# Attention followed by a two-branch maxout layer: wide loads for a second batch, masks by matmul for the first, and scores of two steps issued together

## The chip, the cores and the metric

The kernel runs on one core of one Trainium2 chip. The metric is the device time in microseconds (us), as the median of several executions. "Span" is the time from the first to the last instruction of one profiled execution. Every kernel here computes correct results, and the ratios compare its fast runs alone; a run counts as slow when it is over 1.5% above the fastest of the same kernel.

In the lines of the profile, PE is TensorE (matmuls) and PEld its weight loads, DVE is VectorE, ACT ScalarE, POOL GpSimd, and SPq the queue in which SyncE issues DMAs. PEclk, the granted clock, is the share of TensorE's full clock that it was given. PSUM is the memory into which matmuls write. L522 is line 522 of the kernel.

## The reference, cut to what matters

```python
# q, k, v: 4 batches x 8 heads x 768 tokens x 64; heads 0, 2, 6 are "retrieval" heads
scores = q @ k.T / sqrt(64)
mask   = causal                                        # retrieval heads
mask   = causal & (key < 4 | query - key < 64)         # the five streaming heads
a      = softmax(where(mask, scores, -1e9))
x      = (a @ v) with the heads side by side           # 3072 tokens x 512
out    = maximum(x @ w1, x @ w2) @ w_out               # 512 -> 1024 -> 512
```

## The kernel before

The maxout is rewritten as relu(x(w1 - w2)) w_out + x(w2 w_out). `wd` is the weight difference and `wm` the weight product, both made once on the chip. Four stages run for each batch: loads and transposes of q and k, attention for four pairs of heads, a transpose of the result, and the dense layer. A planner in Python (a list scheduler with estimated costs) fixes, before the program is built, the order in which each engine issues its work. So the order is static, and changing an estimate or a buffer count can reorder everything behind it.

q and k of batch 0 are loaded "wide" (six consecutive tokens a partition) and transposed on TensorE. Later batches are loaded narrow and transposed by the DMA:

```python
order, rate = ("(p n)", 0.34) if b == 0 and src is not v else ("(n p)", 0.225)
... nc.sync.dma_start(out=t.t[:, h], in_=src[b, head].rearrange(f"o {order} d -> p (o n) d", p=128))
...
if b > 0:
    tk.append(P.op(lambda e: nc.sync.dma_start_transpose(out=qk.t..., in_=qb.t...), {"SP": XBAR}, cast, ...))
```

Scores of one step of a pair of heads use 64 rows of the array, one head in the upper and one in the lower half, so that both stream at once. All else uses 128 rows. The exp runs on ScalarE and the mask is multiplied in on VectorE:

```python
for st in range(max(map(len, plans))):
    sc = Buf(sc_p)                                   # 2 buffers of two PSUM banks
    def score(e, ...):
        ... nc.tensor.matmul(sc.t[:, h, off:off + w], lhsT=qk.t[64*h:64*h+64, 1, ...],
                             rhs=qk.t[64*h:64*h+64, 0, q0:q0 + w], start=True, stop=True, ...)
    so.rows = 64
    ... nc.scalar.activation(out=view(a.t...), in_=view(sc.t...), func=ACT.Exp, scale=scale, ...)
    ... V.tensor_mul(out=x, in0=x, in1=m)            # the mask
    ... nc.tensor.matmul(po[h].t[...], lhsT=a.t[...], rhs=vb.t[:, h, j, :], ...)   # values
```

A dense result goes from PSUM through one of three result buffers to memory. The store is issued by the same in-order queue (SyncE) as all loads and all transposing DMAs:

```python
ot_t = tl("ot", [128, d_model], F32, 3)
...
o = P.op(lambda e, bk=bk, ot=ot: copy(e, ot.t, bk.t[:, 0]), {"ACT": 0.53, "DVE": 0.69}, ...)
P.op(lambda e, ot=ot, r0=r0: nc.sync.dma_start(out=out[r0:r0 + 128, :], in_=ot.t), {"SP": 0.45}, [o], [ot], prio=-10, ...)
```

Of the kernel before, what the change touches and what calls it, by code (L numbers as in the profile page):

```python
# [17 lines left out]
class Op:  # L18
    __slots__ = ("emit", "cost", "deps", "bufs", "prio", "size", "rate", "left", "users",
                 "ready", "engine", "start", "end", "done", "rows", "then")  # L20

    def __init__(self, emit, cost, deps, bufs, prio, size, rate):
        self.emit, self.cost, self.deps, self.bufs = emit, cost, deps, bufs
        self.prio, self.size, self.rate = prio, size, rate
        self.left = 0
        self.users = []
        self.ready = 0.0
        self.engine = self.start = self.end = self.done = None
        self.rows, self.then = 128, None
# [24 lines left out]
class Plan:  # L54
# [12 lines left out]
    def schedule(self):  # L67
# [3 lines left out]
        dma = 0.0  # L71
# [26 lines left out]
        while todo:  # L98
# [23 lines left out]
            if e == "PE":  # L122
                o.end += SWITCH if o.rows != rows else 0.0
                rows = o.rows
# [32 lines left out]
W_PRIO = 2.5  # L157
XBAR = 2.6
# [3 lines left out]
def kernel(  # L162
# [69 lines left out]
    warm = tl("warm", [128, 1], F32)  # L232
    tri = tl("tri", [128, 128])
    smk = tl("smk", [128, 448 + 320])
    w2_bf = tl("w2_bf", [128, KC, d_ff])
# [27 lines left out]
    gt_t = [old(2, 1, FC, GT), old(0, 0, FC, GT), old(0, 1, FC, GT)]  # L263
# [11 lines left out]
    def load_weight(name, c):  # L275
        dst, arr, n = {"w1": (w_raw[0], moe_w1, KC // 4), "w2": (w_raw[1], moe_w2, KC // 4),
                       "wo": (w_raw[2], moe_w_out, FC // 4)}[name]
        nc.sync.dma_start(out=dst[:, c * n:(c + 1) * n, :],
                          in_=arr[c * 128 * n:(c + 1) * 128 * n, :].rearrange("(c p) f -> p c f", p=128))

    EARLY = (("wo", 0), ("wo", 1), ("wo", 2), ("wo", 3), ("w2", 0), ("w2", 1))
    with tc.manual_schedule():
# [9 lines left out]
        nc.scalar.activation(out=warm, in_=one[:, 0:1], func=ACT.Exp, scale=1.0, bias=0.0)  # L292
# [51 lines left out]
    def run(full, head, col, exact):  # L344
# [7 lines left out]
        if exact:  # L352
# [5 lines left out]
            c_m = P.op(f, {"DVE": 1.0}, prio=-20)  # L358
# [13 lines left out]
        for i, name in enumerate(("w2", "w1")):  # L372
            for c in range(4):
                d_w[name, c] = None if (name, c) in EARLY else P.op(
                    lambda e, name=name, c=c: load_weight(name, c), {"SP": 0.5},
                    prio=W_PRIO + 0.1 * i + 0.01 * c, size=0.524, rate=0.36)
        wd_ops, w2_ops, wo_ops, wm_ops, w2t_ops = [], [], [], [], []
        for c in range(4):
            w2_ops.append(P.op(lambda e, c=c: copy(e, w2_bf[:, c, :], w_raw[1][:, c, :]),
                               {"DVE": 0.62, "ACT": 0.95}, [d_w["w2", c]], prio=40 + c))  # L380
# [3 lines left out]
        for c in range(4):  # L384
            def f(e, c=c):
                (V if e == "DVE" else nc.gpsimd).tensor_sub(
                    out=wd_bf[:, c, :], in0=w_raw[0][:, c, :], in1=w_raw[1][:, c, :])
            wd_ops.append(P.op(f, {"DVE": 1.3, "POOL": 2.4}, [d_w["w1", c], d_w["w2", c]], prio=48 + c))
        for fch in range(FC):
# [7 lines left out]
            o = P.op(tr, {"PE": 0.23}, w2_ops, [bk], prio=300 + fch)  # L397
# [52 lines left out]

        def attend(b, p, qk, vb, tk, ov, sink, r):
# [12 lines left out]
            for st in range(max(map(len, plans))):  # L464
                hs = [h for h in range(2) if st < len(plans[h])]
                pr = r + 0.1 * st
                steps = {h: plans[h][st] for h in hs}
                same = len(hs) == 2 and plans[0] is plans[1]
                sc = Buf(sc_p)
                at = Buf(as_p[st] if plans[hs[0]] is BAND else at_p)  # L470
                at2 = Buf(as_p[st]) if len(hs) == 2 and not same else at
                where = {hs[0]: at, hs[-1]: at2}

                def score(e, hs=hs, steps=steps, sc=sc):
                    for i in range(max(len(steps[h][1]) for h in hs)):
                        for h in hs:
                            if i < len(steps[h][1]):
                                j, q0, w, off = steps[h][1][i]
                                nc.tensor.matmul(sc.t[:, h, off:off + w],  # L479
                                                 lhsT=qk.t[64 * h:64 * h + 64, 1, j * 128:(j + 1) * 128],  # L480
                                                 rhs=qk.t[64 * h:64 * h + 64, 0, q0:q0 + w],
                                                 start=True, stop=True, skip_group_check=True)
                cols = max(sum(g[2] for g in steps[h][1]) for h in hs)
                so = score_op(score, cols / 2400 + 0.01, tk, [qk, sc], pr)
                so.rows = 64
                ready = {}
                for group in ([hs] if same else [[h] for h in hs]):
                    h0, nh = group[0], len(group)
                    kind, segs, n, diag = steps[h0]
                    a = where[h0]  # L490
                    view, n = region(kind, n)
                    pointer = kind in ("far", "far0")
                    deps = [so] + ([c_m] if pointer else [])
                    for one_ in ([[h] for h in group] if pointer else [group]):
                        def ex(e, a=a, sc=sc, h=one_[0], m=len(one_), view=view, kind=kind):
                            bias = {"far0": bias_0, "far": bias_j}.get(kind)
                            nc.scalar.activation(out=view(a.t[:, h:h + m]), in_=view(sc.t[:, h:h + m]),  # L497
                                                 func=ACT.Exp, scale=scale,
                                                 bias=0.0 if bias is None else bias[:, s0 + h:s0 + h + 1])
                        o = exp_op(ex, n * len(one_), pointer, deps, [sc, a], pr)  # L500
                        ready.update({h: [o] for h in one_})
                    if not pointer:
                        def mk(e, a=a, h0=h0, nh=nh, kind=kind, diag=diag):
                            for x, m in mask_pieces(kind, diag, a.t[:, h0:h0 + nh], nh, s0 + h0):
                                V.tensor_mul(out=x, in0=x, in1=m)  # L505
                        w = (128 * len(diag) if kind == "tri" else n) * nh
                        o = P.op(mk, {"DVE": w * 0.00056 + 0.2}, [o, c_m], [a], prio=pr)
                        ready.update({h: [o] for h in group})
                for h in hs:
                    def av(e, h=h, a=where[h], segs=steps[h][1]):  # L510
                        for (j, q0, w, off) in segs:
                            for t in range(-(-w // 128)):
                                i = q0 // 128 + t
                                nc.tensor.matmul(po[h].t[:, 0, i * (D + 1):(i + 1) * (D + 1)],  # L514
                                                 lhsT=a.t[:, h, off + t * 128:off + (t + 1) * 128],
                                                 rhs=vb.t[:, h, j, :], **flag_of(h))
                    n_av = sum(-(-g[2] // 128) for g in steps[h][1])
                    prev[h] = P.op(av, {"PE": 0.031 * n_av}, ready[h] + [prev[h], ov], [where[h], vb] + (po if prev[h] is None else [po[h]]),
                                   prio=100 + pr)
                if st == 2 and sink is not None:  # L520
                    sunk = sink()
            out_ops = []  # L522
            for h in range(2):
                if not full[s0 + h]:
                    ats, vs, o = sunk
# [6 lines left out]
                    prev[h] = P.op(av, {"PE": 0.13}, [o, prev[h]], [ats, po[h], vs], prio=100 + r + 0.7)  # L532
# [13 lines left out]
        def blk(t):  # L546
            return t.rearrange("c (n p) -> c p n", p=128)

        def pair(b, p):
# [5 lines left out]
            for i, src in enumerate((q, k, v)):  # L555
                t = Buf(ld)
                raws.append(t)
                order, rate = ("(p n)", 0.34) if b == 0 and src is not v else ("(n p)", 0.225)
# [10 lines left out]
            for i in range(2):  # L569
# [3 lines left out]
                cast.append(P.op(f, {"POOL": 0.95, "DVE": 0.62} if r < 1 else {"POOL": 0.95}, loads[i],  # L573
                                 [raws[i], qb], prio=r + 0.01 * i))
                if b > 0:
# [9 lines left out]
                tk.append(P.op(lambda e, bk=bk, i=i: copy(e, tok(qk.t[:, i]), blk(bk.t[:, 0].bitcast(BF16)[:, 0:S])),  # L585
                               {"DVE": 0.95, "ACT": 0.8}, [o], [bk, qk], prio=r))
            if b > 0:
# [7 lines left out]
            ov = P.op(fv, {"POOL": 0.95}, loads[2],  # L595
# [3 lines left out]
            if not (full[s0] and full[s0 + 1]):  # L599
                ks, vs, sc, ats = Buf(ks_p), Buf(vs_p), Buf(sc_p), Buf(sk_p)  # L600
# [11 lines left out]
                def sink():  # L612
                    o = score_op(lambda e: nc.tensor.matmul(sc.t[:, 0, 0:S - 256], lhsT=ks.t, rhs=qk.t[:, 0, 256:S],
                                                            start=True, stop=True, skip_group_check=True),
# [142 lines left out]
```

## Time and profile before

| | before |
|---|---|
| median of the 3 runs | 213.56 us (212.2 to 213.75) |
| span of the profiled run, mean granted TensorE clock | 211.9 us, 0.932 |
| first matmul, last matmul | 13.46 us, 204.8 us |
| TensorE busy | 176.6 us (83%) |

The busy line of the profile's page (engine, busy us, share of the span, instructions) and the first line of its chain of work that ended last (share of the span by engine):

```profile
PE 176.6 (83%) x1460; PEld 94.4 (45%) x1460; DVE 80.1 (38%) x202; ACT 115.9 (55%) x196; POOL 68.2 (32%) x161
...
PE 69%; DVE 8%; ACT 4%; issue 4%; DVEq 0%; ACTq 0%
```

Over the whole span no other engine comes near TensorE, and the chain runs through TensorE for two thirds of the time. A share of 83% hides, however, that the missing 17% lie in three places (start, an early thin stretch, one dip) and that "busy" time at a slow clock also counts as busy. The prediction takes these apart by stretches.

### The profile page before, as it was taken

What the parts mean: (1) busy time and instruction counts of PE and PEld (TensorE: products, weight loads), DVE (VectorE), ACT (ScalarE), POOL (GpSimd) and SP (SyncE); (2) the same over time, 40 slices, a digit from 0 to 9 for tenths busy, and PEclk for the clock granted to TensorE, in tenths of its full rate; (3) what the DMA queues carried; (4) which work ended last, traced back from release to release, by engine and by line L of the source; (5) the groups of instructions that cost most, each with busy time, mean ns of one, the idle gap of its engine ahead of it and who ended that gap; (6) DMA issues with size and microseconds to landing.
All of it is one profiled execution on the core that took longest, in us unless ns stands there. A gap on an engine that the chain in (4) does not pass through costs nothing.

```text
span 211.9 us, 4178 instructions
## 1 busy us (share of the span) xinstructions
PE 176.6 (83%) x1460; PEld 94.4 (45%) x1460; DVE 80.1 (38%) x202; ACT 115.9 (55%) x196; POOL 68.2 (32%) x161
## 2 busy tenths in 40 slices
PE   0038864689799999997879999999999999999960
PEld 0024641545445446545455454545554554545420
DVE  6523799935524563515662035364700000000000
ACT  2088894137385875649553476878472442725320
POOL 6007769929801476243282406120000000000000
PEclk9999996599999999999556999999999999999995
DMA  5999999999999999999999999951183202112030
GB/s 167 404 321 314 357 391 246 221 200 227 209 180 209 236 178 247 242 203 225 192 260 235 232 180 218 212 120 54 49 152 101 99 0 99 53 49 99 14 114 34
DMA packets 99118, 38.91 MB, mean 184 GB/s; under 512 B 91920, under 2 KB 93968, under 8 KB 99088
## 3 DMA queue, kind: packets, MB, share of 16 engines
q1 hardware_dynamic: 99088, 38.55, 82.2%
q8 instruction: 13, 0.21, 0.4%
q14 instruction: 17, 0.14, 0.2%
HBM read 25.17 MB, written 6.29 MB: 148 GB/s over the span
## 4 chain that ended last, share of the span: by engine, by line
PE 69%; DVE 8%; ACT 4%; issue 4%; DVEq 0%; ACTq 0%
PE mm L655 15%; PE mm L673 12%; PE po L514 6%; PE sc L479 6%; PE mm L679 6%; PE po L673 5%; PE sc L655 3%; PE mm L406 3%; DVE at L505 3%; PE po L655 2%; PE po L679 2%; PE sc L673 2%; DVE as_all L505 2%; ACT at L497 2%; ACT as_all L497 2%
## 5 line engine op out<-in xcount | busy, mean ns | idle before, releaser
L497 ACT ACTIVATE at<-sc 128x1024 bf16<-128x1024 f32 (+3 forms) x48 | 33.7, 743 | 7.1 <-PE sc L479 6.5
L655 PE MATMUL mm<-xt,wd_bf 128*128 128x384 bf16 x180 | 35.1, 338 | 0.1
L273 POOL CAST qb<-ld 128x384 bf16<-128x384 f32 x60 | 32.1, 573 | 3.8 <-DMA ld<-in_q_dram 2.0
L655 PEld LDWEIGHTS <-wd_bf 128*128 128x128 bf16 x256 | 24.8, 100 | 18.9 <-issue 4.3
L497 ACT ACTIVATE as_all<-sc 128x896 bf16<-128x896 f32 (+5 forms) x36 | 24.5, 711 | 8.9 <-PE sc L479 8.7
L673 PE MATMUL mm<-wo_bf,raw 128*128 128x512 bf16 x120 | 29.4, 379 | 0.0
L273 POOL CAST vb<-ld 128x384 bf16<-128x384 f32 x32 | 16.2, 533 | 38.6 <-PE po L514 17.1
L505 DVE TENSOR_TENSOR as_all<-as_all,smk 128x384 bf16<-128x384 bf16 (+4 forms) x44 | 20.8, 498 | 20.6 <-ACT as_all L497 20.1
L479 PE MATMUL sc<-qk 64*128 64x192 bf16 (+4 forms) x216 | 25.0, 295 | 2.9 <-ACT as_all L497 1.2
L673 PEld LDWEIGHTS <-raw 128*128 128x128 bf16 x192 | 17.7, 98 | 19.6 <-issue 0.7
L662 ACT ACTIVATE raw<-mm 128x384 bf16<-128x384 f32 x37 | 18.2, 493 | 12.5 <-PE mm L655 11.5
L505 DVE TENSOR_TENSOR at<-at,tri 128x256 bf16<-128x256 bf16 (+1 forms) x48 | 17.1, 364 | 17.4 <-ACT at L497 17.3
L514 PE MATMUL po<-vb,at 128*128 128x65 bf16 x252 | 15.8, 204 | 4.3 <-DVE at L505 4.3
L271 ACT COPY ot<-mm 128x512 f32<-128x512 f32 x14 | 8.2, 587 | 19.8 <-PE mm L679 17.4
L538 DVE TENSOR_TENSOR xs<-po,rz 128x384 f32 x32 | 17.8, 557 | 1.5 <-DVE rz L537 0.4
L582 PE MATMUL mm<-ident,qb 128*128 128x128 bf16 x48 | 5.4, 268 | 14.2 <-DVE qb L273 13.8
L479 PEld LDWEIGHTS <-qk 64*128 64x128 bf16 x216 | 9.3, 97 | 16.7 <-issue 12.8
L514 PEld LDWEIGHTS <-at 128*128 128x128 bf16 x252 | 11.5, 104 | 11.5 <-DVE at L505 7.0
L514 PE MATMUL po<-vb,as_all 128*128 128x65 bf16 x220 | 13.3, 206 | 3.4 <-DVE as_all L505 3.3
L679 PE MATMUL mm<-wm_bf,xt 128*128 128x512 bf16 x60 | 15.4, 380 | 0.0
L514 PEld LDWEIGHTS <-as_all 128*128 128x128 bf16 x220 | 10.5, 105 | 8.9 <-DVE as_all L505 4.8
L679 PEld LDWEIGHTS <-xt 128*128 128x128 bf16 x96 | 8.7, 98 | 9.9 <-issue 0.4
(75 smaller groups left out, 169.4 us busy)
## 6 DMA issues: line engine op xcount, KB each, us to landing
ld<-in_q_dram SPq DMA_DIRECT2D x32, 192.0 KB, 4.3
ld<-in_k_dram SPq DMA_DIRECT2D x32, 192.0 KB, 4.3
ld<-in_v_dram SPq DMA_DIRECT2D x32, 192.0 KB, 4.2
out_dram<-ot SPq DMA_DIRECT2D x24, 256.0 KB, 2.0
raw<-in_moe_w_dram SPq DMA_DIRECT2D x8, 512.0 KB, 7.8
raw<-in_moe_w_out_dram SPq DMA_DIRECT2D x4, 512.0 KB, 5.4
qk<-qb SPq DMA_TRANSPOSE x12, 4.9
xt<-xs SPq DMA_TRANSPOSE x6, 3.8
```

What stands on the lines that cost most here:

```text
L271: nc.scalar.copy(out=o, in_=i)
L273: (V if e == "DVE" else nc.gpsimd).tensor_copy(out=o, in_=i)
L406: nc.tensor.matmul(bk.t[:, 0], lhsT=w2t[:, f, c * 128:(c + 1) * 128], rhs=wo_bf[:, f, :], start=(f == 0), stop=(f == FC - 1))
L479: nc.tensor.matmul(sc.t[:, h, off:off + w], lhsT=qk.t[64 * h:64 * h + 64, 1, j * 128:(j + 1) * 128], rhs=qk.t[64 * h:64 * h + 64, 0, q0:q0 ...
L497: nc.scalar.activation(out=view(a.t[:, h:h + m]), in_=view(sc.t[:, h:h + m]), func=ACT.Exp, scale=scale, bias=0.0 if bias is None else bia ...
L505: V.tensor_mul(out=x, in0=x, in1=m)
L514: nc.tensor.matmul(po[h].t[:, 0, i * (D + 1):(i + 1) * (D + 1)], lhsT=a.t[:, h, off + t * 128:off + (t + 1) * 128], rhs=vb.t[:, h, j, :], ...
L538: V.tensor_tensor(out=xs[b].t[:, :, bass.ds(col(s0 + h), D)], in0=p3[:, :, 0:D], in1=rz.t.unsqueeze(2).to_broadcast([128, NB, D]), op=ALU. ...
L655: nc.tensor.matmul(bk.t[:, 0, 0:GT], lhsT=wd_bf[:, c, f * 128:(f + 1) * 128], rhs=xt[b].t[:, g * NB // NG:(g + 1) * NB // NG, c, :], start ...
L662: nc.scalar.activation(out=gt.t[:, f, :], in_=bk.t[:, 0, 0:GT], func=ACT.Relu)
L673: nc.tensor.matmul(bk.t[:, 0], lhsT=gt.t[:, f, t * 128:(t + 1) * 128], rhs=wo_bf[:, f, :], start=(f == 0), stop=False)
L679: nc.tensor.matmul(bk.t[:, 0], lhsT=xt[b].t[:, c0 // 128, c, :], rhs=wm_bf[:, c, :], start=False, stop=(c == KC - 1))
```

## The change

The intent: start earlier by moving weights behind activations; take the mask off VectorE while it is crowded (batch 0); get q and k of batch 1 sooner; and pay the 64-row mode switch once for two score steps. The core of the diff, with cuts:

```diff
+WIDE_TO, MASK_TO, X_BAR, DUO_FROM = 2, 1, 1, 1
 ...
-    gt_t = [old(2, 1, FC, GT), old(0, 0, FC, GT), old(0, 1, FC, GT)]
+    gt_t = [tl("gt", [128, FC, GT]), old(2, 1, FC, GT), old(0, 0, FC, GT)]
 ...
-    EARLY = (("wo", 0), ("wo", 1), ("wo", 2), ("wo", 3), ("w2", 0), ("w2", 1))
+    EARLY = (("wo", 0), ("wo", 1), ("wo", 2), ("wo", 3))
+    LATER = {("w2", 0): 1.5, ... ("w1", 0): 3.5, ...}         # weights by quarters, later
 ...
-                order, rate = ("(p n)", 0.34) if b == 0 and src is not v else ("(n p)", 0.225)
+                order, rate = ("(p n)", WIDE) if b < WIDE_TO and src is not v else ("(n p)", NARROW)
 ...
-                if b > 0:
+                if b >= WIDE_TO:                                # else six transposes on TensorE
                     continue
 ...
-            for st in range(max(map(len, plans))):
-                sc = Buf(sc_p)
+            size = 2 if b >= DUO_FROM else 1
+            by_pe = exact and b < MASK_TO
+            for g0 in range(0, len(tiles), size):
+                group = tiles[g0:g0 + size]
+                scs = [Buf(sc_p) for _ in group]                # one issue, one or two buffers
+                def score(e, group=group, scs=scs):
+                    for x, sc in zip(group, scs):
+                        ...                                     # scores, 64 rows, as before
+                        for k, h, st in heads if by_pe else []:
+                            for o, m in negatives(plans[h][st]):
+                                nc.tensor.matmul(sc.t[:, k, o:o + m.shape[-1]], lhsT=ident, rhs=m,
+                                                 start=False, stop=True, skip_group_check=True)
```

A mask by matmul adds a large negative number to the masked scores in PSUM (identity times a matrix of zeros and negatives), so the exp makes them zero. The four constants are switches, by batch number: batches below `WIDE_TO` load wide, batches below `MASK_TO` mask by matmul, batches from `DUO_FROM` on group their score steps.

## The prediction

> **What bounds the kernel now.** I read the page's slice view first, then busy time by stretches, then timelines of the two thin stretches, then the chain of waits. Slices (5.3 us each; busy tenths; PEclk is the granted clock of TensorE):
>
> ```profile
> PE   0038864689799999997879999999999999999960
> DVE  6523799935524563515662035364700000000000
> PEclk9999996599999999999556999999999999999995
> DMA  5999999999999999999999999951183202112030
> ```
>
> TensorE is nearly always busy from slice 10 on, with one dip at slices 18 and 19. The clock fell twice, each time just after TensorE thinned out. The DMA row is full for two thirds of the span and then falls away while TensorE stays full: the end is set by TensorE. Stretches, cut at the first matmul, at the start of the dense stage of batch 0 and around the dip (after the length: busy us of PE, PEld, DVE, ACT, POOL, then granted clock, DMA share, GB/s):
>
> ```profile
> 0.00:13.50 13.50, 0.04 (x1) 0.04 (x2) 7.01 (x24) 4.05 (x5) 3.49 (x18) 1.00 0.84 301
> 13.50:56.60 43.10, 32.52 (x331) 19.57 (x332) 28.71 (x52) 25.81 (x41) 32.22 (x59) 0.88 1.12 273
> 56.60:93.00 36.40, 36.38 (x326) 18.58 (x326) 15.93 (x44) 23.94 (x41) 15.48 (x39) 1.00 1.19 212
> 93.00:118.00 25.00, 21.10 (x189) 11.96 (x187) 11.33 (x32) 15.43 (x27) 9.26 (x23) 0.73 1.19 231
> 118.00:154.00 36.00, 35.81 (x354) 18.47 (x353) 17.06 (x51) 24.26 (x41) 7.77 (x24) 1.00 0.79 147
> 154.00:205.00 51.00, 50.76 (x266) 25.73 (x263) 0.06 (x1) 21.98 (x44) 0.00 (x0) 1.00 0.27 78
> ```
>
> So the time is: start 13.5 us without matmuls, TensorE work at full clock, TensorE losses, a tail of 7.1 us from the last matmul (ends 204.8) to 211.9, and 1.7 us from the span to the median of 213.56. Losses: 13.5 to 56.6 has 10.6 us idle and about 3.3 us of slow clock (busy 7.87 us at 0.77 from 25 to 40, 14.83 us at 0.90 from 40 to 56.6); 93 to 118 has 3.9 us idle and 21.10 x 0.27 = 5.7 us of slow clock; the rest 0.4 us. Sum 23.9 us, so the work is 204.8 - 13.5 - 23.9 = 167.4 us.
>
> Why the first loss, from the timeline (start, length, engine, line, operation, count, idle before it):
>
> ```profile
> 29.26 6.96 POOL L386 TENSOR_TENSOR wd_bf<-raw 128x1024 bf16<-128x1024 f32 x3
> 29.65 4.33 DVE L505 TENSOR_TENSOR at<-at,tri 128x128 bf16<-128x128 bf16 x2
> 31.74 0.30 PE L514 MATMUL po<-vb,at 128*128 128x65 bf16 x4 [1.51 <-DVE at L505]
> 36.16 3.37 POOL L273 CAST qb<-ld 128x384 bf16<-128x384 f32 x4
> ```
>
> While GpSimd subtracts weights, two mask multiplications that otherwise take 0.22 us each take 4.33 us together; the value matmuls wait for them; and the casts of pair 3 stand behind the subtractions until 36.2 though its loads were issued from 23.1. The scores of pair 3 come at 47.2 and dense work only at 56.6.
>
> Why the second: the last normalization of batch 1 ends at 90.5, but the transposes of its result are far back in the one in-order DMA-issuing queue:
>
> ```profile
> 89.95 0.56 DVE L538 TENSOR_TENSOR xs<-po,rz 128x384 f32 x1
> 100.15 3.78 SPq L588 DMA_TRANSPOSE qk<-qb  x1
> 105.28 1.80 SPq L628 DMA_TRANSPOSE xt<-xs  x1
> 111.23 8.11 PE L655 MATMUL mm<-xt,wd_bf 128*128 128x384 bf16 x36
> ```
>
> Dense work of batch 0 was used up at about 95, that of batch 1 starts at 111.2.
>
> **What the Trainium skill says.** "TensorEngine Tiling (Array Packing)", Key Properties: a change of tiling mode drains TensorE. The chain agrees and gives the size:
>
> ```profile
> 62.89 0.32 PE sc L479 x2
> 63.22 0.76 PE mm L655 x4
> ...
> 153.53 0.65 PE mm L655 x4
> ```
>
> Two concurrent 512-column scores take 0.32 us where 512 columns stream in 0.216 us (eight L673 matmuls in 1.73 us), and four L655 matmuls behind them take 0.76 in place of 0.65: 0.11 us in and 0.11 us out, 0.22 us an excursion. "GPSIMD Engine Reference", section 1 (Specifications): its SBUF interface is shared with VectorE, with contention for instructions with two SBUF inputs; the 4.33 us above agree. "DMA: Bandwidth & Descriptors", Specifications: transfers under 512 B do not reach line rate. A narrow row here is 64 floats, 256 B; a wide one is six tokens, 1536 B. From 4 to 31 us (weights, wide q and k, narrow v) the DMA view shows 358 GB/s, from 31 to 54 us (narrow only) 224 GB/s: agrees. "TensorE: Matmul & The Clock Gate", Part 1: an idle window of about 3.4 us halves the clock; here the granted clock falls after both thin stretches, though no single gap is that long.
>
> **The change part by part.**
>
> Start. Two of the six early weight loads (1.05 MB, at about 0.36 MB/us 2.9 us) move behind pair 1. The first q load is issued at 6.7 in any case (head order), but lands behind less. First matmul at about 10.8 instead of 13.5: **-2.7 us**.
>
> Masks of batch 0 by matmul. Removed: the multiplications of batch 0 on VectorE, a wait between exp and value matmuls. Added on TensorE: full heads have 6 diagonal blocks of 128 columns (768), streaming heads 448+384+320 = 1152. Three full and five streaming heads make 8064 columns x 0.42 ns (0.216 us over 512) = **+3.4 us**. They use 128 rows, which mostly follow a score anyway, so I count no more switches.
>
> Wide q and k of batch 1. 3.15 MB at about 0.37 instead of 0.22 MB/us: 8.5 instead of 14.3 us of DMA, and four DMA transposes with 2.4 to 3.8 us of issue time each leave the issuing queue. Added: eight groups of six transposes on TensorE at about 0.5 us (0.50 us at 45.4), **+4.0 us**, and eight PSUM copies of 0.80 (ScalarE) or 0.96 us (VectorE), on engines under 70% busy there. The DMA gain itself is off the end's path; it counts only through the second loss.
>
> Scores of two steps together, batches 1 to 3. Before, a batch makes 6+6+3+3 = 18 excursions; after 3+3+2+2 = 10. 3 x 8 x 0.22 = 5.3 us; one merged tile in batch 0 adds 0.2: **-5.5 us**.
>
> Weight subtraction by quarters, later (behind the loads of batch 0), dense groups that wait for the right half only, an own buffer for the first dense result, VectorE allowed for all casts of batch 0. Bytes up to the last weight: 2.1 + 4.7 + 4.2 = 11 MB as before, landed at about 33. Pair 3 has its data at about 28, its first score at 31; from first score to dense was 9.4 us (47.2 to 56.6), so dense work can start at about 40 instead of 56.6, and the weight product (32 matmuls, about 7 us) no longer needs an empty TensorE. The work of batch 0 that belongs before 40 (167.4 less the 138 us after 56.6, plus masks: 32 us) fits barely between 10.8 and 40; I choose 7 us of loss in place of 13.9: **-6.9 us**.
>
> Second dip. Batch 1 is ready some 15 us earlier relative to the queue, so dense work should not run out there. But the transposes of batch 2 stand in the same queue behind the narrow loads and transposes of batch 3, and a group of two steps needs both score buffers free at once, so the exps of one group no longer overlap the scores of the next. I choose 3.5 us of loss left out of 9.6, plus the 0.4: **-6.1 us**.
>
> Sum: -2.7 + 3.4 + 4.0 - 5.5 - 6.9 - 6.1 = -13.8, so 213.56 - 13.8 = 199.8; I write **199.5 us**.
>
> **Rivals.** (1) The planned order is static, and it slips: TensorE waits for exps because both score buffers must be free, or for the two mm buffers that transposes of batch 1 now share with dense work. For it: in 93 to 111 scores already waited 0.17 to 0.72 us each for exps. Against: elsewhere dense matmuls stand between and the idle is 0.2 us in 36. 30 groups at 0.3 us would be 9 us: about 207 to 209. (2) The dip only moves to batch 2, with its slow clock: all 9.6 us stay, about 206. (3) All gaps close: losses of 3 us instead of 10.9, about 191 to 192. For it: the DMA share falls sooner and batches 2 and 3 are as before. (4) Loads bound batch 0 wholly; TensorE waits as long as now and only the start, the dip and the switches count: about 205. Slower by 2% would need TensorE stalls beyond 18 us over my sum; I see no source for it.
>
> **Range and chances.** The work is known to about 2 us, the losses only to about 6: range 191.5 to 207. Faster by over 2% means under 209.3; rivals 1, 2 and 4 alone stay under it, two together might not. Faster 0.93, same 0.06, slower 0.01.
>
> **What would show it.** First matmul at 10 to 11.5; first L655-type matmul at 38 to 44; no multiplications by masks before then; value matmuls after an exp without a wait for VectorE; eight qk transposes by DMA instead of twelve; TensorE without a dip in the stretch after batch 0's dense work; four-step score groups with one switch; TensorE busy rising from 83 to about 88%. Wrong if the first dense matmul comes after 48, if a second dip with a slow clock stays, or if scores wait over 5 us in all for exps.

## The result and the profile after

| | before | after |
|---|---|---|
| median of 4 runs | 213.19 us (212.2 to 213.75) | 202.38 us (201.31 to 205.73) |
| ratio of the fast runs | | 0.9481 (95%: 0.942 to 0.9543) |
| span, mean granted clock | 211.9 us, 0.932 | 200.4 us, 0.984 |
| first matmul, last matmul | 13.46, 204.8 us | 10.89, 193.3 us |

Ratios here and below are the mean time of one kernel's fast runs over the mean of the other's fast runs of the same rounds, so they differ a little from the ratio of the quoted medians. One of the four runs of after (205.73 us) was over 1.5% above the fastest and is left out of the ratio as slow (the median of the other three is 202.15 us); the profiled run was a fast one. The change is faster by 5.2%, 2.9 us above the predicted point and inside the range.

The slice view of the changed kernel (5.0 us a slice, the same rows as in the prediction):

```profile
PE   0049988987999999999999399999999999999950
DVE  5555494756596823466304224755400000000000
PEclk9999999999999999999999969999999999999996
DMA  4999999999999999999999999802192102113120
```

TensorE is dense from slice 4 on, and one slice is thin, the 23rd, with one slow clock right behind it. Both broad losses of before have shrunk. By stretches (columns as in the prediction's second fence):

```profile
20.00:54.00 34.00, 30.96 (x403) 19.80 (x400) 21.27 (x45) 25.46 (x39) 21.69 (x49) 1.00 1.06 302
54.00:76.00 22.00, 21.67 (x227) 12.26 (x224) 14.48 (x39) 14.89 (x27) 13.31 (x32) 1.00 1.09 209
76.00:111.00 35.00, 34.51 (x320) 18.33 (x320) 14.24 (x40) 22.64 (x38) 13.19 (x33) 1.00 1.17 219
111.00:120.00 9.00, 5.65 (x36) 2.13 (x32) 2.55 (x7) 2.80 (x4) 3.06 (x8) 0.81 1.22 242
```

The length less the first busy column is TensorE's idle time: 3.04, 0.33, 0.49 and 3.35 us. From 10.9 to 20 it is 1.94 us, and after 120 next to nothing: 9.2 us together. The slow clock costs 5.65 x 0.19 = 1.1 us in the last of these rows. So the losses went from 23.9 to 10.3 us, the start from 13.5 to 10.9 us, and the work at full clock is 193.3 - 10.9 - 10.3 = 172.1 us, against 167.4 us before. Those three moves, -13.6, -2.6 and +4.7, are the 11.5 us between the spans; the tail of 7.1 us did not change.

One slow clock is in none of these columns. The trace holds no clock record before 19.85 us (22.78 in before), and the views show 1.00 where there is none. Until then a two-matmul score takes 0.61 us, and 0.39 us from 20.01 on. If all TensorE work slowed alike, that costs some 2.5 us of the 7.02 us busy until then in after, and 2.8 of 7.89 us in before (estimates from these numbers). Both sums count it as work, so it hardly changes the difference.

The busy line and the chain's first line:

```profile
PE 173.2 (86%) x1546; PEld 95.2 (48%) x1546; DVE 77.2 (39%) x205; ACT 114.1 (57%) x188; POOL 58.3 (29%) x149
...
PE 56%; DMA 22%; SPq 5%; DVE 4%; issue 3%; ACT 3%; POOL 3%; ACTq 0%; POOLq 0%; DVEq 0%
```

TensorE is a larger share of a shorter span, yet the chain goes through TensorE less than before, and through the DMA for 22%. A chain that leaves the busiest engine says that something else set a date. Where it does is the thin slice; the timeline of it (start, length, engine, line, operation, count, idle before it and its releaser):

```profile
109.12 0.59 SPq L741 DMA_DIRECT2D out_dram<-ot  x1
...
109.81 2.56 SPq L649 DMA_TRANSPOSE qk<-qb  x1
...
113.83 0.59 ACT L274 COPY ot<-mm 128x512 f32<-128x512 f32 x1 [3.59 <-DMA out_dram<-ot]
...
114.47 2.68 PE L728 MATMUL mm<-wo_bf,raw 128*128 128x512 bf16 x8 [3.35 <-ACT ot L274]
```

A store of a dense result is issued at 109.12. In the chain of waits it lands 4.63 us later, and the two steps ahead of it are the casts of a later pair on GpSimd (106.10 to 108.48), then a load that the queue issues with their end. ScalarE can copy the next result only into the buffer that this store frees, TensorE's dense matmuls need the PSUM buffer that this copy frees, and 3.35 us pass. So, as the trace reads, the gap that is left comes from result buffers and the order of one issuing queue, not from late transposes as in the dip of before; run 7 tests the buffers.

In the early stretch, the first scores of pair 3 and the first dense matmul:

```profile
36.07 0.37 PE L522 MATMUL sc<-qk 64*128 64x256 bf16 x4
...
54.06 0.82 PE L709 MATMUL mm<-xt,wd_bf 128*128 128x384 bf16 x4
```

Pair 3 comes 11 us sooner than before (47.2). The first dense matmul comes only 2.5 us sooner (56.6), but TensorE is hardly waiting: between the two it is busy 16.35 of 17.99 us and works off the weight product, the q and k transposes of batch 1 and the first scores of batch 1.

### The profile page after: what moved, and what is told of

It reads as the page before. It is cut to its first block, busy times and chain, and to the rows that moved or that the text cites. A ratio compares the mean times of both kernels' runs of the same rounds, so it can differ in the third digit from the quotient of the medians.

```text
span 200.4 us, 4316 instructions
## 1 busy us (share of the span) xinstructions
PE 173.2 (86%) x1546; PEld 95.2 (48%) x1546; DVE 77.2 (39%) x205; ACT 114.1 (57%) x188; POOL 58.3 (29%) x149
## 4 chain that ended last, share of the span: by engine, by line
PE 56%; DMA 22%; SPq 5%; DVE 4%; issue 3%; ACT 3%; POOL 3%; ACTq 0%; POOLq 0%; DVEq 0%
PE mm L728 8%; PE mm L709 8%; DMA ld<-in_v_dram 8%; PE sc L522 6%; DMA qk<-qb 5%; PE sc L728 5%; PE po L579 4%; SPq L621 4%; PE mm L734 4%; PE mm L420 4%; DMA raw<-in_moe_w_dram 3%; PE po L709 3%; PE sc L709 3%; PE po L728 3%; PE sc L734 3%
## 5 line engine op out<-in xcount | busy, mean ns | idle before, releaser
L550 ACT ACTIVATE at<-sc 128x1024 bf16<-128x1024 f32 (+3 forms) x44 | 33.4, 790 | 10.3 <-PE sc L522 6.1
L276 POOL CAST qb<-ld 128x384 bf16<-128x384 f32 x52 | 27.3, 555 | 18.4 <-DMA ld<-in_k_dram 8.0
L522 PE MATMUL sc<-qk 64*128 64x192 bf16 (+4 forms) x216 | 22.5, 287 | 2.0 <-ACT qk L274 1.6
L642 PE MATMUL mm<-ident,qb 128*128 128x128 bf16 x96 | 9.1, 242 | 13.8 <-DVE qb L276 11.9
L728 PEld LDWEIGHTS <-raw 128*128 128x128 bf16 x120 | 11.6, 98 | 16.6 <-issue 4.3
L728 PE MATMUL mm<-wo_bf,raw 128*128 128x512 bf16 x64 | 16.4, 393 | 3.4 <-ACT ot L274 3.4
L564 DVE TENSOR_TENSOR as_all<-as_all,smk 128x384 bf16<-128x384 bf16 (+4 forms) x33 | 14.8, 473 | 10.5 <-ACT as_all L550 10.4
L642 PEld LDWEIGHTS <-qb 128*128 128x128 bf16 x96 | 7.2, 109 | 15.6 <-DVE qb L276 12.2
L717 ACT ACTIVATE raw<-mm 128x384 bf16<-128x384 f32 x23 | 11.3, 491 | 5.4 <-PE mm L709 4.9
L579 PE MATMUL po<-vb,at 128*128 128x65 bf16 x252 | 13.9, 197 | 0.0
L734 PEld LDWEIGHTS <-xt 128*128 128x128 bf16 x96 | 9.0, 99 | 10.3 <-issue 1.1
L728 PE MATMUL mm<-wo_bf,gt 128*128 128x512 bf16 x56 | 13.7, 379 | 0.0
L579 PEld LDWEIGHTS <-at 128*128 128x128 bf16 x252 | 11.5, 100 | 3.9 <-issue 1.5
L564 DVE TENSOR_TENSOR at<-at,tri 128x256 bf16<-128x256 bf16 (+1 forms) x36 | 9.6, 288 | 8.7 <-ACT at L550 8.6
```

What stands on the lines that cost most here:

```text
L276: (V if e == "DVE" else nc.gpsimd).tensor_copy(out=o, in_=i)
L522: nc.tensor.matmul(sc.t[:, k, off:off + w], lhsT=qk.t[64 * h:64 * h + 64, 1, j * 128:(j + 1) * 128], rhs=qk.t[64 * h:64 * h + 64, 0, q0:q0 ...
L550: nc.scalar.activation(out=view(a.t[:, k:k + m]), in_=view(sc.t[:, k:k + m]), func=ACT.Exp, scale=scale, bias=0.0 if bias is None else bia ...
L564: V.tensor_mul(out=y, in0=y, in1=m)
L579: nc.tensor.matmul(po[h].t[:, 0, i * (D + 1):(i + 1) * (D + 1)], lhsT=a.t[:, k, off + t * 128:off + (t + 1) * 128], rhs=vb.t[:, h, j, :], ...
L642: nc.tensor.transpose(psb[:, n * 128:(n + 1) * 128], qb.t[:, i, n].rearrange("p h d -> p (h d)"), ident)
```

## The experiments

Twelve kernels ran, in three groups of four, each timed in 3 rounds beside the kernel before (medians of the kernel before in the three groups: 212.44, 212.62 and 212.98 us). "After" without more is the changed kernel. A warning for all switches: the planner makes a new static order for each of them, so an edit of one part also moves other work. Three edits avoid this, as they change only what is emitted in a place of the order (split groups and doubled masks).

### 1. Masks of batch 0 back on VectorE

```diff
-WIDE_TO, MASK_TO, X_BAR, DUO_FROM = 2, 1, 1, 1
+WIDE_TO, MASK_TO, X_BAR, DUO_FROM = 2, 0, 1, 1
```

> The changed kernel with the masks of batch 0 multiplied on VectorE again. My theory: the mask matmuls cost 3.4 us of TensorE, but VectorE's masks stood in the way of the value matmuls only while GpSimd subtracted weights, and the subtraction now comes after nearly all of the masks; so undoing this part alone changes little: 200 to 204 us (202.4 now), with less TensorE work before 50 us and more waits for VectorE. Rival: the masks on VectorE are what kept TensorE idle; then the waits for VectorE come back and it takes 206 us or more.

Measured: 206.09 us (204.35 to 206.5), ratio 0.9667 (0.9595 to 0.9739), 3.9 us slower than after by the ratios (0.0186 x 212). My theory fell; the rival held, just inside its range. One stretch by the window view, then four masks on VectorE and the value matmuls that wait for them:

```profile
40.00:50.00 10.00, 7.86 (x43) 3.70 (x42) 5.32 (x6) 0.76 (x2) 9.88 (x17) 0.53 1.08 287
```

```profile
38.06 5.85 DVE L564 TENSOR_TENSOR as_all<-as_all,smk 128x896 bf16<-128x896 bf16 x4
...
43.96 0.51 PE L579 MATMUL po<-vb,as_all 128*128 128x65 bf16 x6 [2.14 <-DVE as_all L564]
```

From 20 to 40 us TensorE is busy 6.82 and 5.90 of each 10 us, then the granted clock falls to 0.53. GpSimd is busy for nearly the whole of the stretch shown, and subtracts weights from 38.80 to 43.56: against the theory, four masks still meet the subtraction, as in before, and the longest of these masks takes 2.62 us. The longest wait of TensorE there, 2.32 us at 38.77, is for GpSimd itself. So the masks by matmul do pay for their TensorE time, by closing part of the early loss.

The other runs bear this out. From 10.9 to 60 us TensorE is idle 13.4, 10.5 and 11.3 us in the three kernels with the masks of batch 0 on VectorE (runs 1, 4 and 10), and 5.3, 4.7 and 3.9 us in after and runs 2 and 3, with masks by matmul, whatever the other switches are.

### 2. No grouping of score steps

```diff
-WIDE_TO, MASK_TO, X_BAR, DUO_FROM = 2, 1, 1, 1
+WIDE_TO, MASK_TO, X_BAR, DUO_FROM = 2, 1, 1, 4
```

> The changed kernel with one step for each score excursion everywhere. My theory: 24 more excursions at 0.22 us, TensorE busy 5.3 us more and the time 206 to 208.5 us. Rival: with single steps the scores of one step overlap the exps of the other, so that fewer waits give most of it back: 202 to 204 us.

Measured: 198.51 us (197.34 to 201.3), ratio 0.9305 (0.923 to 0.938). The slowest of the four runs is a slow one. Theory and rival both missed, and by the sign: without grouping the kernel is 3.7 us faster than after by the ratios. Counting in the traces how often TensorE goes into 64-row matmuls and out again (an excursion) gives 55 before (14, 14, 13 and 14 by batch), 47 after (17, then 10 in each later batch) and 57 here, of which 40 in batches 1 to 3. So single steps do not make 18 excursions a batch, as the prediction had read from the code. The planner itself puts two steps back to back in places. The stretch with the gap, after first, then this kernel:

```profile
105.00:140.00 35.00, 31.65 (x303) 16.16 (x302) 16.20 (x46) 20.56 (x34) 8.47 (x24) 0.95 0.84 180
```

```profile
105.00:140.00 35.00, 32.46 (x331) 16.91 (x331) 17.43 (x51) 20.94 (x35) 8.46 (x23) 1.00 0.90 180
```

Here the gap is 0.8 us smaller and does not cost clock (1.1 us after). With 0.5 us less idle from 10.9 to 60 and 0.5 us less from 60 to 105, that makes 2.9 of the 3.5 us between the spans (196.9 and 200.4); the rest is not assigned. The gap's matmul still waits 2.08 us for the copy behind a store.

### 3. Narrow loads for batch 1

```diff
-WIDE_TO, MASK_TO, X_BAR, DUO_FROM = 2, 1, 1, 1
+WIDE_TO, MASK_TO, X_BAR, DUO_FROM = 1, 1, 1, 1
```

> The changed kernel with batch 1 loaded narrow and transposed by DMA again. My theory: the eight groups of transposes (4 us of TensorE) go, but batch 1 comes later and the DMA-issuing queue holds four more transposes, so that a gap with a slow clock of 5 to 12 us opens where dense work of batch 0 ends, between 75 and 110 us: 205 to 210 us. Rival: the load mattered little, and without the transposes on TensorE it is faster than now: 198 to 201 us.

Measured: 211.31 us (210.74 to 211.71), ratio 0.9928 (0.9868 to 0.9988). The theory held in what it said of the gap, though the time is 1.3 us above its range: nearly the whole gain is gone. Two stretches and one line of the table of waits (total us, times, longest):

```profile
90.00:100.00 10.00, 5.91 (x55) 3.03 (x55) 2.95 (x9) 5.44 (x7) 3.34 (x10) 0.50 1.10 241
100.00:110.00 10.00, 6.46 (x63) 3.90 (x63) 4.97 (x17) 5.06 (x10) 5.11 (x15) 0.50 1.18 236
```

```profile
PE sc L522 <- DMA qk<-qb: 8.2, 4, 3.0
```

TensorE is busy about 60% of these 20 us at half the clock. Over the whole run its scores wait 8.2 us for the transposing DMAs, at most 3.0 us at a time. From 84.3 to 115 us the granted clock is 0.50 with 20.68 us of busy time, so the slow clock, with 10.3 us, cost more than these waits.

### 4. All three switches off, the rest kept

```diff
-WIDE_TO, MASK_TO, X_BAR, DUO_FROM = 2, 1, 1, 1
+WIDE_TO, MASK_TO, X_BAR, DUO_FROM = 1, 0, 1, 4
```

> The changed kernel without all three named parts: what is left is the order of the weight loads, their quarters, casts on VectorE in batch 0, the own buffer of the dense result and the tiles of the pair with one full head. My theory: the earlier start gives 2.6 us, and the later subtraction of weights most of the early loss of 14 us back, while the second gap of 9.6 us stays: 203 to 208 us, TensorE's first matmul at 10.9. Rival: the three named parts do the work, and this takes 209 to 213 us.

Measured: 214.55 us (213.1 to 215.17), ratio 1.0099 (1.0037 to 1.0162), slower than before by 1%, which is the same by the 2% that count here; both missed. The earlier start and the later weights alone gain nothing. From 90 to 110 TensorE is busy 6.96 and 6.18 of each 10 us at clocks of 0.63 and 0.50, with 4.5 us of waits for the transposing DMAs. The early loss did not go either: from 10.9 to 60 us TensorE is idle 10.5 us and the clock is 0.93. So only the earlier start is won, and it is given back in the same dip as in run 3.

### 5. Every group split again, in the same order

Before the second step of each of 21 groups a matmul of one column with 128 rows takes TensorE out of the 64-row mode and back. Nothing else moves.

```diff
-                    for x, sc in zip(group, scs):
+                    for pos, (x, sc) in enumerate(zip(group, scs)):
 ...
+                        if pos and heads:
+                            nc.tensor.matmul(sc.t[:, 0, 0:1], lhsT=ident, rhs=ident[:, 0:1],
+                                             start=True, stop=True, skip_group_check=True)
```

> The changed kernel in its own order, with one matmul of one column on 128 rows put between the two steps of each score group: 21 groups of batches 1 to 3 are split. My theory: two switches of 0.11 us and some 0.05 us for the matmul itself, 21 x 0.27 = 5.7 us more TensorE time, nearly all of it on the path since TensorE has under 2 us of idle there besides one gap: 206.5 to 209 us, against 202.4. Rival: a switch costs nothing of its own (the 0.11 us are the drain of the last matmul, which the modelled ends only show there): 202 to 204 us.

Measured: 201.1 us (200.51 to 201.33), ratio 0.9457 (0.9432 to 0.9481). Theory and rival both missed: it takes no longer than after. The cost is there, however. The same group in after, then here:

```profile
78.98 0.61 PE L522 MATMUL sc<-qk 64*128 64x512 bf16 x6
79.52 0.54 PE L579 MATMUL po<-vb,at 128*128 128x65 bf16 x12
```

```profile
80.47 0.39 PE L525 MATMUL sc<-qk 64*128 64x512 bf16 x2
80.79 0.18 PE L518 MATMUL sc<-ident 128*128 128x1 bf16 x1
80.90 0.39 PE L525 MATMUL sc<-qk 64*128 64x128 bf16 x4
81.22 0.54 PE L582 MATMUL po<-vb,at 128*128 128x65 bf16 x12
```

From the first score to the value matmuls 0.54 us became 0.75 us, so a split costs 0.21 us, the inserted matmul included. (No run put in a matmul of 64 rows, which would leave the mode as it is, so the share of the switch alone is not isolated; the prediction read 0.22 us an excursion from before's chain, without any inserted matmul.) Where did 21 of them go? This kernel from 105 to 140 us, beside after's row in run 2:

```profile
105.00:140.00 35.00, 34.44 (x322) 17.66 (x326) 16.75 (x48) 22.60 (x37) 8.00 (x24) 1.00 0.88 174
```

TensorE arrives later and the gap is gone, idle 0.56 in place of 3.35 us. The gap's end was a date set by a store, so TensorE time ahead of it was free.

### 6. Every mask matmul of batch 0 issued twice

```diff
-nc.tensor.matmul(sc.t[:, k, o:o + m.shape[-1]], lhsT=ident, rhs=m, start=False, stop=True, ...)
+for again in range(2):
+    nc.tensor.matmul(sc.t[:, k, o:o + m.shape[-1]], lhsT=ident, rhs=m, start=False, stop=again == 1, ...)
```

> The changed kernel in its own order, with each of the 38 mask matmuls of batch 0 issued twice. Theory from the prediction: 8064 columns x 0.42 ns = 3.4 us, partly at the slow clock of the first 9 us, and TensorE is nearly full from 20 us on: 3.5 to 5 us more, 205.5 to 208 us. Rival: batch 0 waits for its loads and for ScalarE anyway, so TensorE time there is hidden: 202 to 204 us.

Measured: 202.15 us (201.45 to 203.09), ratio 0.9508 (0.9468 to 0.9548). The rival's time held, but not its reason. The first dense matmul, at 54.06 us in after, and the wait at the gap:

```profile
57.48 0.82 PE L710 MATMUL mm<-xt,wd_bf 128*128 128x384 bf16 x4
...
115.23 1.89 PE L729 MATMUL mm<-wo_bf,raw 128*128 128x512 bf16 x8 [1.06 <-ACT ot L274]
```

The second copy was not hidden in batch 0: dense work starts 3.4 us later, what the theory gave for 8064 columns. It was the gap that took it up, as in run 5: the wait of 3.35 us shrank to 1.06 us. What a mask matmul costs on its own can therefore not be read from the time of the changed kernel.

### 7. Seven result buffers

The change had left half of a dead raw weight unused; four result buffers fit there. (A fourth buffer of its own does not fit: that build needed 209.8 kB of the 207.9 kB a partition has for it, and did not run.)

```diff
-    ot_t = tl("ot", [128, d_model], F32, 3)
+    ot_t = tl("ot", [128, d_model], F32, 3) + [raw[:, 0, 2048 + d_model * i:2048 + d_model * (i + 1)] for i in range(4)]
```

> The changed kernel with seven result buffers for the stores in place of three (four of them in the room of weights that are no longer needed). My theory: the gap at 111 us, where a copy of a result waits 3.6 us for the store of an earlier one and TensorE stands 3.35 us and then runs 5.7 us of work at 0.81 of the clock, goes: 197.5 to 200 us. Rival: TensorE then meets the next lack, dense work of batch 2 which is not ready, and stands as long: 201.5 to 203.5 us.

Measured: 197.93 us (197.52 to 198.3), ratio 0.9317 (0.9297 to 0.9337). The theory held. The longest wait of TensorE after 60 us is now

```profile
114.36 0.61 PE L522 MATMUL sc<-qk 64*128 64x512 bf16 x6 [0.82 <-DMA qk<-qb]
```

No matmul waits for a result copy there. The planner made a new order here too, but the issuing queue keeps after's order up to 116 us, past the gap: the same store is issued, at 107.75 us, and no copy around it waits for a store. This shows that the gap at 111 us came from the result buffers.

### 8. Seven result buffers and no grouping

The edits of runs 2 and 7 together.

> Single score steps everywhere (as in the faster run before) and seven result buffers. In that run a copy waited 5.2 us for a store and TensorE stood 2.1 us at 111 us. My theory: 195 to 197.5 us (198.5 with three buffers). Rival: the room is taken by another lack: 198 to 199.5 us.

Measured: **195.6 us** (194.58 to 195.98), ratio 0.9186 (0.9156 to 0.9215), span 194.2 us, clock 0.994. The theory held, and this version beats both kernels. From 60 to 120 us no wait of TensorE is long enough for the timeline to mark. Single steps are ahead of grouped ones here too, by 2.3 us by the medians, so their advantage in run 2 was not only a smaller gap. Half of the 1.6 us between the spans is the 0.82 us wait of run 7; where the rest lies is open, as a few matmul records (16 and 18) are missing from these two traces.

### 9. Seven result buffers, groups split

The edits of runs 5 and 7 together: the same order as run 7, with 21 splits.

> The changed kernel with seven result buffers (197.9 us, hardly a gap left) and its 21 score groups split by a one-column matmul. Each split took 0.21 us of TensorE in the trace of the split run. My theory: it was hidden there behind the gap at 111 us, which the store sets; without that gap 3 to 4.4 us of the 21 x 0.21 show: 200.5 to 202.5 us. Rival: TensorE time between 60 and 140 us is not what sets the end at all: 197.5 to 199 us.

Measured: 200.81 us (200.46 to 201.84), ratio 0.944 (0.9375 to 0.9505). The theory held. With the gap closed, the splits show: 2.9 us more than run 7 by the medians, out of 21 x 0.21 = 4.4 us. Together with run 5 this settles that a split is a real cost and that after's gap had hidden it.

### 10. Wide loads alone

```diff
-WIDE_TO, MASK_TO, X_BAR, DUO_FROM = 2, 1, 1, 1
+WIDE_TO, MASK_TO, X_BAR, DUO_FROM = 2, 0, 1, 4
```

> Of the three named parts only the wide loads of batch 1 (masks on VectorE, single steps). Without all three it took 214.6 us. My theory: the wide loads bring batch 1 forward and close the gap with the slow clock that the kernel without them has from 90 to 112 us: 202 to 206 us; so they are the main part. Rival: each part works only with the others: 208 to 213 us.

Measured: 204.01 us (201.98 to 205.53), ratio 0.9608 (0.9529 to 0.9687). One of the four runs is a slow one. The theory held: from 80 to 110 us TensorE is busy for all 30.00 us at a clock of 1.00. Against run 4, which differs only in this switch, it is 10.4 us faster by the ratios. The early loss stays: from 10.9 to 60 us TensorE is busy 37.77 us, against 43.85 us after.

### 11. Stores issued by ScalarE

On top of run 8:

```diff
-nc.sync.dma_start(out=out[r0:r0 + 128, :], in_=ot.t), {"SP": 0.45}, ...
+nc.scalar.dma_start(out=out[r0:r0 + 128, :], in_=ot.t), {"ACT": 0.1}, ...
```

> Single steps, seven result buffers, and the stores issued from ScalarE's queue in place of the common one. Theory: stores no longer stand behind loads, but with seven buffers nothing waits for them any more (no wait for a store in the trace of the run before), so 195 to 196.5 us, the same as without[...]. Rival: the common queue is what orders the loads of batches 2 and 3, and without 24 stores in it they come earlier: 192.5 to 194.5 us.

Measured: 200.44 us (199.83 to 200.63), ratio 0.941 (0.9351 to 0.9469). Both missed: 4.8 us slower than run 8. A new gap opens earlier:

```profile
80.56 1.03 PE L522 MATMUL sc<-qk 64*128 64x512 bf16 x6 [3.38 <-DMA qk<-qb]
```

Its cause is not a new order of the queue: up to 89 us SyncE issues the same loads and transposing DMAs in the same order as in run 8, without the stores. But two q loads that take 1.25 us of the queue in run 8 (from 69.77) take 4.86 us here (from 69.71), and the first transposing DMA of batch 2 is issued at 74.73 instead of 71.19. SyncE's own waits from 60 to 85 us have one line that run 8 has not:

```profile
SPq L621 <- DMA out_dram<-ot: 3.8, 1, 3.8
```

The second of these loads stands until a store that ScalarE issued at 72.00 has landed; in the trace it waits for, and then uses, the semaphore of that store. So the store still stood in the way of the loads, by a semaphore instead of a queue. That this one wait makes up the whole 4.8 us is not shown. An issue held ScalarE's queue for 0.34 us, where the edit gave the planner 0.1 us; what that costs stays open.

### 12. Wide loads for batch 2 too

On top of run 8:

```diff
-WIDE_TO, MASK_TO, X_BAR, DUO_FROM = 2, 1, 1, 4
+WIDE_TO, MASK_TO, X_BAR, DUO_FROM = 3, 1, 1, 4
```

> Single steps, seven result buffers, and batch 2 loaded wide and transposed on TensorE too. Theory: TensorE has under 0.5 us of idle between 60 and 143 us (195.6 us), so the eight groups of six transposes at 0.42 us more are added nearly whole: 197.5 to 200 us. Rival: batch 2 and 3 come earlier and that helps the order of work: 194 to 195.5 us.

Measured: 201.81 us (201.06 to 202.2), ratio 0.9469 (0.9409 to 0.9528), 6.2 us slower than run 8. The direction held, the size did not. Run 8 first, then this one:

```profile
60.00:90.00 30.00, 29.89 (x284) 15.98 (x284) 15.41 (x43) 20.01 (x34) 14.73 (x35) 1.00 1.16 214
```

```profile
60.00:90.00 30.00, 29.09 (x377) 17.15 (x374) 27.11 (x66) 24.39 (x40) 20.85 (x49) 1.00 1.07 228
```

The transposes and copies of batch 2 now lie in the dense stretch. TensorE is busy 177.9 us in place of 171.3 over the span, and VectorE nearly always from 60 to 90. The theory had counted the transposes alone: they take 13.0 us in place of 8.8, and there are 62 excursions in place of 56. Wide loads pay where TensorE would otherwise wait for the data (batch 1) and cost where it would not.

## Why the prediction was right or wrong

The time was right: 202.38 us against 199.5 us, in the range, and faster by over 2%. Its bound was right too: TensorE with its losses. Part of the nearness is luck, as misses of both signs cancel: the early loss shrank by 2.0 us more than predicted and the second dip by 1.4 us less, and the work at full clock rose by 2.8 us more. Two of the prediction's own three signs of being wrong came true, the late first dense matmul and a second dip with a slow clock; the third did not. Step by step:

- **Start, -2.7 us: right.** Measured -2.57 us. Alone it is worth nothing (run 4): it counts only because the dip behind it is closed.
- **Masks, +3.4 us on TensorE: right in size, but free here.** Doubling them delayed the first dense matmul by 3.4 us and changed nothing in the time (run 6). Taking them away cost 3.9 us (run 1). The prediction put the gain of the masks into the early loss, and that is where run 1 lost it. Its "no more switches" was wrong: batch 0 has 17 excursions in place of 14.
- **Wide q and k of batch 1: right, and the largest part.** The prediction said that the DMA gain counts only through the second dip. Narrow loads brought the dip back with its slow clock and 9.5 us by the ratios (run 3); wide loads alone took off 10.4 us (run 10 against run 4). The transposes on TensorE take 9.1 us in place of 5.4, 3.7 us more where +4.0 was predicted.
- **Scores of two steps together, -5.5 us: this step failed.** "Before, a batch makes 6+6+3+3 = 18 excursions" counted steps in the code. The trace of before has 13 or 14, since its planner already pairs steps. In batches 1 to 3 the change saves 11 excursions, not 24, and batch 0 makes 3 more, since its masks part the steps: 8 x 0.21 = 1.7 us in place of 5.5 us. That shortfall of 3.8 us is about the size of the whole miss of 2.9 us, and lies where the sum is off: work at full clock rose by 4.7 us, where +3.4 + 4.0 - 5.5 = +1.9 us was predicted. (With 1.7 in place of 5.5 it would be +5.7; the 1.0 us between is not assigned.) The size of one excursion was right (0.21 us by run 5, 0.22 us predicted). The worry that a group needs both score buffers free fits runs 2 and 8, in which single steps are 3.7 and 2.3 us faster than groups. But no run shows that wait by itself, and the table of waits of after lists only 0.2 us in which scores wait for exps. So why groups are slower remains open.
- **Early loss 13.9 to 7 us: larger gain than predicted, by another way.** Measured 1.94 + 3.04 = 5.0 us idle with no recorded slow clock. The prediction booked this gain under the later subtraction, the own buffer and the casts. These alone did not bring it (run 4: 10.5 us idle), and all three kernels without masks by matmul kept it (run 1). The step "dense work can start at about 40" failed: it starts at 54.06, beyond the 48 that the prediction had named as a sign against itself. Its own numbers were against it: 32 us of work do not fit "barely" into the 29.2 us between 10.8 and 40. TensorE filled the time with the weight product and batch 1's transposes and scores instead, so the date of the first dense matmul did not matter.
- **Second dip 9.6 to 3.5 us, plus 0.4: the size was near, the cause was not.** Measured 4.2 us idle after 54 us and 1.1 us of slow clock. The gap that stayed was put down beforehand to late transposes and score buffers. It came from three result buffers and the wait for a store (run 7); how much of that wait is due to the shared issuing queue no run isolates. This is rival 2 in part: a smaller dip with its slow clock moved to a later place.
- **TensorE busy about 88%: near,** 86% measured.

Of the rivals, 1 (stalls on exps: 9 us) fell, with 0.2 us of such waits listed, and so did 4 (loads bound batch 0 wholly). Rival 3 (all gaps closed) became true only with more result buffers and no grouping, and then at 195.6 us rather than 191 to 192.

## What to carry to other kernels

Count mode switches in the trace, not in the loop that issues the work: a planner may already have merged some of them (here 18 steps a batch were 13 or 14 excursions), and forced groups were 2 to 4 us slower here than single steps, for a reason that stayed open. If a wait's end is a date set elsewhere, here by a store, any work ahead of it looks free and any saving ahead of it looks worthless; close that gap first, then measure. A few more result buffers in dead memory were worth some 4 us here, where the grouping saved nothing.

## What the Trainium skill lacked or had wrong

- "TensorEngine Tiling (Array Packing)", Key Properties, says that a change of tiling mode drains TensorE, and gives no size. Here one excursion to another mode costs 0.21 us (0.75 against 0.54 us, run 5, with the inserted one-column matmul in it; 0.22 us by before's chain).
- "TensorE: Matmul & The Clock Gate", Part 1, names in its table of states an idle window of about 3.4 us as the way to half the clock. In run 3 waits of at most 3.0 us with work between them were enough for a granted clock of 0.50 over 20 us, with TensorE busy about 60%. In before the clock fell to 0.50 at 101.3 us after TensorE had been busy 6.70 of 8.30 us, with no wait over 0.50 us among them. The same part also tells of a kernel whose frequent short idles made the clock go back and forth; it gives no length for them.
- "DMA: Bandwidth & Descriptors", Issuing engines are not separate DMA queues, says that issuing usually takes little next to the DMA itself. A transposing DMA of q and k held the issuing queue for 2.52 us here, of 4.6 us to its landing (medians of eight in after).
